# Decayed causal attention and a GELU MLP: one attention-times-values run per head pair, masks of batch 1 on GpSimd, and half a key block left out

## The chip, the cores and the metric

One core of a Trainium2 chip. The metric is the device time in microseconds (us) of one execution; "span" is the time from the first to the last instruction in a profile, 2 to 3 us less. Engines are TensorE (PE; its weight loads PEld), VectorE (DVE), ScalarE (ACT), GpSimd (POOL) and SyncE (SP), which issues transfers.

## The reference

```python
# q, k, v: (8 batches, 8 heads, 576, 64); f: (8, 8, 576)
scores = q @ k.T / sqrt(64)
cum = cumsum(log(clip(f, 1e-4, 1)))
scores = where(causal, -1e9, scores + cum[:, None] - cum[None, :])
attn = softmax(scores) @ v
x = attn.transpose(0, 2, 1, 3).reshape(8 * 576, 512)
out = gelu_exact(x @ w_in) @ w_out          # 512 -> 2048 -> 512
```

The decay is folded into v: each key's row of v is weighed by exp(-cum) and a 65th column carries the weights, so that softmax is a division by that column.

## The kernel before

Heads are worked on in pairs: a batch has pairs 0 to 3, each of two heads in the two halves of the partitions. A pair has four score tiles, scores(pair, 0..3), each followed by one exp on ScalarE and, from batch 2 on, by causal masks on GpSimd. "AV" is attention times values, 15 matmuls a head. A "bank" is a buffer in PSUM, the memory to which TensorE's results go; a matmul that needs a bank waits until the last user of it is done. Between these, TensorE takes single steps ("fill") of the second GEMM of the batch before.

```python
STILES = [
    [(0, 0, 256), (3, 384, 192)],          # (key block, first query, queries)
    [(0, 256, 320), (4, 448, 128)],
    [(1, 128, 448)],
    [(2, 256, 320)],
]
SDIAG = [[0, 256], [320], [0], [0]]        # columns of the diagonal blocks

s_psum = ctx.enter_context(tc.tile_pool(name="s_psum", bufs=2, space=PSUM))
o_psum = ctx.enter_context(tc.tile_pool(name="o_psum", bufs=2, space=PSUM))

    def scores(b, i, t):
        on_pe = b < 2                       # mask added by matmuls in batches 0 and 1
        st = s_psum.tile([P, 2, 512], FP32, tag="s", name=f"s{t}")
        # ... matmuls of 64 rows, both heads side by side ...
        et = e_pool.tile([P, 2, 512], BF16, tag=f"e{t}", name=f"e{t}")
        nc.scalar.activation(et[:, :, 0:c], st[:, :, 0:c], Act.Exp, scale=scale)
        for c0 in [] if on_pe else SDIAG[t]:
            nc.gpsimd.affine_select(out=et[:, :, c0 : c0 + P], ...)

    # second GEMM by token tile; "r": two 64-row matmuls side by side, "n": one of 128 rows
    PLAN = [
        (0, "o", 16 * "r"),
        (1, "m", 5 * "r" + 2 * "n" + 8 * "r" + "n"),
        (2, "m", 9 * "r" + 2 * "n" + 5 * "r"),
        (3, "s", 8 * "r" + 8 * "n"),
    ]
    FILL = [[6, 5, 4, 3], [0, 3, 3, 2], [0, 3, 3, 3], [0, 3, 3, 2], [8]]
    FILL_AV = [2, 1, 2, 2]

    def attention(b):                       # batches 2 to 7
        # ...
        counts = FILL_2 if b == 2 else FILL  # FILL_2: another list, not changed
        def av(i):
            for h in range(2):
                attend(b, i, h, (0, 1, 2, 3, 4))
                if h == 0 and (b > 2 or i == HP - 1):
                    take(fill, FILL_AV[i])
                normalize(b, i, h)
        for i in range(HP):
            for t in range(4):
                scores(b, i, t)
                take(fill, counts[i][t])
                if i and t == 1:
                    av(i - 1)
                # ...
                if t == 1 and i == 0:
                    load_v(b + 1)
        take(fill, counts[HP][0])
        if b == 2:
            to_xT(b, HP - 2, nc.vector.tensor_copy, o_psum, "o")
        av(HP - 1)
        take(fill, 5)
        to_xT(b, HP - 1, nc.vector.tensor_copy, o_psum, "o")
        # ...
    # main loop, first GEMM of batch b: v of batch b + 1 is weighed on GpSimd,
    # pair by pair, all four pairs ahead of the masks of batch b + 1
```

The softmax here doesn't subtract the row's maximum and nothing guards it: scores larger than these inputs give would overflow.

Of the kernel before, what the change touches and what calls it, by code (L numbers as in the profile page):

```python
# [9 lines left out]
BF16 = mybir.dt.bfloat16  # L10
Act = mybir.ActivationFunctionType
# [3 lines left out]
P = 128  # L15
S = 576
D = 64
H = 8
HP = 4
NBLK = 5  # L20
K0 = [0, 128, 256, 384, 448]
# [3 lines left out]
PT = 96  # L25


STILES = [
    [(0, 0, 256), (3, 384, 192)],
    [(0, 256, 320), (4, 448, 128)],  # L30
    [(1, 128, 448)],
    [(2, 256, 320)],
]

SDIAG = [[0, 256], [320], [0], [0]]


def where(n, m):

    q = K0[m]  # L40
    for t, parts in enumerate(STILES):
        c = 0
# [8 lines left out]
def kernel(  # L51
# [10 lines left out]
    nc = tc.nc  # L62
# [10 lines left out]
    scale = 1.0 / (D ** 0.5)  # L73
# [3 lines left out]
    consts = ctx.enter_context(tc.tile_pool(name="consts", bufs=1))  # L77
    qk_pool = ctx.enter_context(tc.tile_pool(name="qk", bufs=2))
    v_pool = ctx.enter_context(tc.tile_pool(name="v", bufs=1))
    e_pool = ctx.enter_context(tc.tile_pool(name="e", bufs=4))  # L80
# [50 lines left out]
    key_of = consts.tile([P, 2, P], BF16)  # L131
    after = consts.tile([P, 2, P], BF16)
    for t, op, fill in (
# [4 lines left out]
            out=t[0:D],  # L138
            in_=t[0:D],
            compare_op=op,  # L140
            fill=fill,
            base=0,
            pattern=[[-D, 2], [1, P]],
# [5 lines left out]
    make_identity(nc, ident_fp)  # L149


    qT = [consts.tile([P, S], BF16, name=f"qT{i}") for i in range(HP)]
    kT = [consts.tile([P, S], BF16, name=f"kT{i}") for i in range(HP)]

# [106 lines left out]
    e_of = {}  # L261

    def scores(b, i, t):
        on_pe = b < 2
        st = s_psum.tile([P, 2, 512], FP32, tag="s", name=f"s{t}")
        c = 0
        for n, q0, w in STILES[t]:
            masked = on_pe and c in SDIAG[t]
            for half in range(-1, 2 if masked else 0):
                for h in range(2):  # L270
                    d = slice(h * D, (h + 1) * D)
                    if half < 0:
                        to = st[:, h, c : c + w]
                        ab = kT[i][d, K0[n] : K0[n] + P], qT[i][d, q0 : q0 + w]
                    else:
                        last = (half + 1) * D
                        to = st[:, h, c : c + last]
                        ab = key_of[d, half, :], after[d, half, 0:last]
                    nc.tensor.matmul(  # L279
                        to, *ab, start=half < 0, stop=half == 1 or not masked  # L280
                    )
            c += w
        et = e_pool.tile([P, 2, 512], BF16, tag=f"e{t}", name=f"e{t}")
        e_of[b, i, t] = et
        nc.scalar.activation(et[:, :, 0:c], st[:, :, 0:c], Act.Exp, scale=scale)  # L285
        for c0 in [] if on_pe else SDIAG[t]:
            nc.gpsimd.affine_select(  # L287
                out=et[:, :, c0 : c0 + P],
                in_=et[:, :, c0 : c0 + P],
                compare_op=Alu.is_ge,  # L290
                fill=0.0,
                base=0,
                pattern=[[0, 2], [1, P]],
                channel_multiplier=-1,
            )

# [44 lines left out]
    def x_dma(b, i):  # L341
        nc.sync.dma_start_transpose(
            xT(b)[:, i, :].rearrange("d (m p) -> d m p", p=P),
            x_of[b, i].rearrange("p m h d -> p (m h d)"),
        )
# [31 lines left out]
    def gemm2(c):  # L377
# [35 lines left out]

    PLAN = [
        (0, "o", 16 * "r"),
        (1, "m", 5 * "r" + 2 * "n" + 8 * "r" + "n"),
        (2, "m", 9 * "r" + 2 * "n" + 5 * "r"),
        (3, "s", 8 * "r" + 8 * "n"),
    ]

# [8 lines left out]
    def gemm2_rows(c, plan):  # L429




        for ts, held, steps in plan:
            if held == "s":
                both = s_psum.tile([P, 2, d_model], FP32, tag="s", name="ps2")
                banks = [both[:, 0], both[:, 1]]
            else:
                pool = {"o": o_psum, "m": m_psum}[held]
                banks = [  # L440
                    pool.tile([P, d_model], FP32, tag=held, name="ps2")
                    for _ in range(2)
                ]
            ot = o_pool.tile([P, d_model], FP32, tag="ot", name="ot")
            for kt, step in enumerate(steps):
                last = kt == steps.rindex("r")
                for r in range(2 if step == "r" else 1):
                    rows = slice(r * D, (r + 1) * D) if step == "r" else slice(0, P)
                    nc.tensor.matmul(  # L449
                        banks[r],  # L450
                        g_of[c][kt][rows, ts * P : (ts + 1) * P],
                        w_out_sb[rows, kt, :],
                        start=(kt == 0),
                        stop=last if r else kt == n_ff - 1,
                    )
                if kt == n_ff - 1 if held == "s" else last:
                    nc.vector.tensor_copy(ot, banks[1])  # L457
                if kt == n_ff - 1:
                    nc.vector.tensor_tensor(ot, ot, banks[0], Alu.add)  # L459
                    store(c, ts, ot)  # L460
                yield
# [37 lines left out]
    def gemm2_third():  # L499
        yield from gemm2_half(0, 1)  # L500
        yield from gemm2_rows(0, PLAN_0)
        yield from gemm2_rows(1, PLAN_1)

    def take(gen, n):
        for _ in range(n):
            if next(gen, "end") == "end":
                return
# [89 lines left out]



    FILL = [[6, 5, 4, 3], [0, 3, 3, 2], [0, 3, 3, 3], [0, 3, 3, 2], [8]]  # L600
    FILL_AV = [2, 1, 2, 2]
    FILL_2 = [[8, 8, 8, 8], [8, 8, 4, 4], [4, 4, 4, 4], [4, 4, 4, 4], [8]]
    FILL_1 = [[0, 0, 0, 0], [0, 0, 0, 0], [0, 0, 2, 2], [2, 2, 0, 0], [4]]

    def attention(b):


        fill = gemm2_third() if b == 2 else gemm2_rows(b - 1, PLAN)
        counts = FILL_2 if b == 2 else FILL

        def av(i):
            for h in range(2):
                attend(b, i, h, (0, 1, 2, 3, 4))
                if h == 0 and (b > 2 or i == HP - 1):
                    take(fill, FILL_AV[i])
                normalize(b, i, h)

        for i in range(HP):
# [5 lines that stand above are left out]
                    if i < HP - 1 or b > 2:  # L624
                        x_dma(b, i - 1)
                if t == 1 and i == 0:
                    load_v(b + 1)
                if b > 2 and t == 0 and i < 2:
                    transpose_dma(b + 1, 4 * i, 4 * i + 4)
                if b == 2 and t == 1 and i == 1:  # L630
                    transpose_dma(3, 0, 4)
                    transpose_dma(3, 4, 8)
        take(fill, counts[HP][0])
        if b == 2:
            to_xT(b, HP - 2, nc.vector.tensor_copy, o_psum, "o")
        av(HP - 1)
        take(fill, 5)
        to_xT(b, HP - 1, nc.vector.tensor_copy, o_psum, "o")
        x_tail(b)
        take(fill, 999)  # L640

    def second_attention():


        b, fill = 1, gemm2_half(0, 0)

        def av(i, h):
            attend(b, i, h, (0, 1, 2, 3, 4))
            normalize(b, i, h)

        def transposes(i, pool, tag):
            for which in range(2):
                transposes_first(b, i, which, pool, tag)


        nc.scalar.activation(warm[0:1, 0:1], warm[0:1, 0:1], Act.Exp)
        weigh_v(1, 2)
        weigh_v(1, 3)
# [3 lines that stand above are left out]
                if i == 0 and t < 3:  # L662
                    transposes(t + 1, *((m_psum, "m") if t == 1 else (o_psum, "o")))
                take(fill, FILL_1[i][t])
                if i and t in (1, 2):
                    av(i - 1, t - 1)
                if i > 1 and t == 0:
                    to_xT(b, i - 2, nc.vector.tensor_copy, o_psum, "o")
                if (i, t) == (3, 0):
                    transpose_dma(2, 0, 4)  # L670
                    transpose_dma(2, 4, 8)
        to_xT(b, HP - 2, nc.vector.tensor_copy, o_psum, "o")
        av(HP - 1, 0)
        take(fill, FILL_1[HP][0])
        av(HP - 1, 1)
        both = s_psum.tile([P, 2, 1024], BF16, tag="s", name="ps_x2")
        take(fill, 99)
        gemm1_begin(1, both)
        x_tail(1)
        load_v(2)  # L680
# [69 lines left out]
```

## Time and profile before

| | before |
|---|---|
| time, median of 3 (low to high) | 353.64 us (353.11 to 353.71) |
| span of the profiled run, granted clock | 350.1 us, 0.998 |
| TensorE, ScalarE, VectorE, GpSimd busy | 96%, 62%, 54%, 35% of the span |
| start of scores(0, 0) in batches 1, 2, 3 | 39.97, 74.01, 121.30 us |
| period of batches 3 to 7 | 36.627 us |

The period is the mean of four distances between the first score matmuls of batches 3 to 7.

### The profile page before, as it was taken

To read this page: it belongs to the slowest core of one execution; us is meant where nothing else is said; L and a number is where in the kernel's file an instruction comes from. 1 tells how busy PE (TensorE), PEld (TensorE's weight loads), DVE (VectorE), ACT (ScalarE), POOL (GpSimd) and SP (SyncE) were. 2 spreads that over 40 slices of the span, in tenths; PEclk is the share of its full clock that TensorE was granted. 3 is DMA by queue.
4 is the path that set the end of the run, shared out by engine and by line. 5 is a ranking of instruction groups with operands and counts; after the bars stand their busy time and mean duration, and the time that the engine had idled before them with its cause. 6 is when DMAs were issued, how large, how long until landed. Compare 5 with 4: busy or idle time off the path is not lost.

```text
span 350.1 us, 8011 instructions
## 1 busy us (share of the span) xinstructions
PE 335.7 (96%) x3250; PEld 179.0 (51%) x3292; DVE 188.7 (54%) x424; ACT 215.6 (62%) x296; POOL 122.8 (35%) x237
## 2 busy tenths in 40 slices
PE   7799998999999999999999999999999999999995
PEld 3674565445554455545554455445544554444443
DVE  5670455943367935796469646975498452011011
ACT  5976785673734787468746874687567774603600
POOL 8390740209318044443436242714270530000000
PEclk9999999999999999999999999999999999999999
DMA  8999999993970989278944896299700150011013
GB/s 115 174 171 194 209 186 176 205 190 89 217 187 31 138 184 188 77 100 163 191 122 73 151 222 122 55 160 213 159 30 0 51 98 33 0 60 62 0 32 89
DMA packets 99924, 43.03 MB, mean 123 GB/s; under 512 B 78704, under 2 KB 95344, under 8 KB 99888
## 3 DMA queue, kind: packets, MB, share of 16 engines
q1 hardware_dynamic: 82592, 28.37, 40.4%
q0 software_dynamic: 16896, 13.63, 26.2%
q8 instruction: 25, 0.41, 0.5%
q10 hardware_dynamic: 400, 0.52, 0.4%
q14 instruction: 11, 0.09, 0.1%
HBM read 36.85 MB, written 9.44 MB: 132 GB/s over the span
## 4 chain that ended last, share of the span: by engine, by line
PE 83%; ACT 9%; issue 2%; POOL 2%; DMA 2%; DVE 1%; ACTq 0%; POOLq 0%; DVEq 0%
PE ps L358 35%; PE ps L449 20%; PE o L306 9%; PE ps L391 8%; PE s L279 7%; ACT e L285 5%; PE ps L484 2%; ACT L285 2%; DMA k<-in_k_dram 2%; ACT g L375 1%; PE ps_x L336 1%; POOL q L103 1%; DVE x L320 1%; POOL k L103 1%; PE ps_f L199 0%
## 5 line engine op out<-in xcount | busy, mean ns | idle before, releaser
L375 ACT ACTIVATE g<-ps 128x512 bf16<-128x512 f32 x144 | 85.3, 597 | 78.9 <-PE ps L358 78.9
L285 ACT ACTIVATE e<-s 128x896 bf16<-128x896 f32 (+1 forms) x128 | 104.4, 862 | 31.4 <-PE s L279 30.1
L358 PE MATMUL ps<-xT,w_in_sb 128*128 128x512 bf16 x503 | 111.9, 379 | 0.8 <-ACT ot L493 0.2
L449 PE MATMUL ps<-w_out_sb,g 64*128 64x512 bf16 (+1 forms) x726 | 103.3, 376 | 1.6 <-issue 0.8
L358 PEld LDWEIGHTS <-w_in_sb 128*128 128x128 bf16 x576 | 56.1, 98 | 67.5 <-issue 2.3
L287 POOL TENSOR_SCALAR_AFFINE_SELECT e<-e 128x256 bf16<-128x256 bf16 x120 | 47.6, 408 | 94.2 <-ACT e L285 93.4
L449 PEld LDWEIGHTS <-g 64*128 64x128 bf16 (+1 forms) x751 | 40.0, 94 | 30.8 <-issue 3.3
L279 PE MATMUL s<-qT,kT 64*128 64x320 bf16 (+4 forms) x384 | 47.0, 281 | 4.8 <-ACT e L285 3.4
L237 DVE COPY qT<-tq 64x288 bf16<-64x288 bf16 x96 | 48.5, 506 | 1.7 <-DMA tq<-q 0.3
L253 POOL TENSOR_TENSOR vw<-v_sb,wT 128x640 bf16<-128x640 f32 x31 | 39.7, 1279 | 22.2 <-DMA v_sb<-in_v_dram 22.1
L306 PEld LDWEIGHTS <-e 128*128 128x128 bf16 x960 | 35.7, 98 | 15.7 <-issue 9.1
L306 PE MATMUL o<-vw,e 128*128 128x65 bf16 x960 | 40.7, 194 | 0.7
L457 DVE COPY ot<-ps 128x512 f32<-128x512 f32 x26 | 17.9, 689 | 40.0 <-PE ps L449 40.0
L237 DVE COPY kT<-tk 64x288 bf16<-64x288 bf16 x96 | 33.1, 344 | 1.6
L279 PEld LDWEIGHTS <-kT 64*128 64x128 bf16 x384 | 20.4, 94 | 25.5 <-issue 12.6
L320 DVE TENSOR_TENSOR x<-o,r 128x320 bf16<-128x320 f32 x64 | 31.5, 491 | 2.4 <-DVE r L319 0.2
L400 DVE COPY ot<-ps 128x512 f32<-128x512 f32 (+2 forms) x9 | 5.7, 632 | 48.6 <-PE ps L391 45.8
L319 DVE RECIPROCAL r<-o 128x5 f32<-128x5 f32 x64 | 12.3, 192 | 29.3 <-PE o L306 29.1
L391 PE MATMUL ps<-w_out_sb,g 128*128 128x512 bf16 (+2 forms) x141 | 27.8, 355 | 0.2
L391 PEld LDWEIGHTS <-g 128*128 128x128 bf16 x144 | 13.5, 98 | 14.5
L459 DVE TENSOR_TENSOR ot<-ot,ps 128x512 f32<-128x512 f32 x26 | 17.9, 687 | 1.5
L348 POOL COPY tails<-xT 128x256 bf16<-128x256 bf16 x8 | 3.2, 398 | 41.8 <-DVE xT L339 41.8
(63 smaller groups left out, 164.3 us busy)
## 6 DMA issues: line engine op xcount, KB each, us to landing
out_dram<-ot SPq DMA_DIRECT2D x32, 256.0 KB, 2.2
v_sb<-in_v_dram SPq DMA_DIRECT2D x24, 256.0 KB, 4.8
q<-in_q_dram POOLq DMA_DIRECT2D x6, 576.0 KB, 6.0
k<-in_k_dram POOLq DMA_DIRECT2D x6, 576.0 KB, 8.6
v_sb<-in_v_dram SPq DMA_DIRECT2D x22, 128.0 KB, 5.2
w_in_sb<-in_moe_w_in_dram POOLq DMA_DIRECT2D x4, 512.0 KB, 7.2
w_out_sb<-in_moe_w_out_dram POOLq DMA_DIRECT2D x4, 512.0 KB, 12.0
q<-in_q_dram POOLq DMA_DIRECT2D x4, 144.0 KB, 4.3
```

What stands on the lines that cost most here:

```text
L237: nc.vector.tensor_copy(rows[:, odd], src[odd * D : (odd + 1) * D, 2 * i + h].rearrange("d j p -> d p j"),)
L253: eng.tensor_tensor(vw_of[b][:, hs, :, 0:D], v_sb[:, hs, :, :], w.unsqueeze(3).to_broadcast([P, 2, NBLK, D]), Alu.mult,)
L279: nc.tensor.matmul(to, *ab, start=half < 0, stop=half == 1 or not masked)
L285: nc.scalar.activation(et[:, :, 0:c], st[:, :, 0:c], Act.Exp, scale=scale)
L287: nc.gpsimd.affine_select(out=et[:, :, c0 : c0 + P], in_=et[:, :, c0 : c0 + P], compare_op=Alu.is_ge, fill=0.0, base=0, pattern=[[0, 2], [ ...
L306: nc.tensor.matmul(o[:, m, :], e_of[b, i, t][:, h, c : c + P], vw_of[b][:, 2 * i + h, n, :], start=(n == 0), stop=(n == m),)
L320: nc.vector.tensor_tensor(x_of[b, i][:, :, h, :], o[:, :, 0:D], r.unsqueeze(2).to_broadcast([P, NBLK, D]), Alu.mult,)
L358: nc.tensor.matmul(ps, w_in_sb[:, kt, ffb * P : (ffb + 1) * P], src[:, kt, 0:TC], start=(kt == 0), stop=(kt == n_dm - 1),)
L375: nc.scalar.activation(g_of[c][ffb], ps, Act.Gelu)
L391: nc.tensor.matmul(pss[ts][:, c0:c1], g_of[c][kt][:, ts * P : (ts + 1) * P], w_out_sb[:, kt, c0:c1], start=(kt == 0), stop=(kt == n_ff - 1),)
L449: nc.tensor.matmul(banks[r], g_of[c][kt][rows, ts * P : (ts + 1) * P], w_out_sb[rows, kt, :], start=(kt == 0), stop=last if r else kt == n ...
L457: nc.vector.tensor_copy(ot, banks[1])
```

## The change

Its intent: fewer interruptions of AV, less masking on TensorE, and no work on queries that the last key block never sees. The last block overlaps the one before it by 64 keys, so for its first 64 queries all that would be computed is masked or weighed with zero. Their part of the tile becomes constant zeros.

```diff
-    [(0, 256, 320), (4, 448, 128)],
+    [(4, 448, 128), (0, 256, 320)],
-SDIAG = [[0, 256], [320], [0], [0]]
+SDIAG = [[0, 256], [0], [0], [0]]
+    e4 = [consts.tile([P, 2, 448], BF16, name=f"e4{i}") for i in range(4)]
+    for t in e4:
+        nc.gpsimd.memset(t[:, :, 0:D], 0.0)
     def scores(b, i, t):
-        on_pe = b < 2
+        on_pe = b == 0 or (b == 1 and i == 0)
+            z = D if n == NBLK - 1 else 0
-                        to = st[:, h, c : c + w]
+                        to = st[:, h, c + z : c + w]
     # ... the operands and the masks by matmul likewise; et of t == 1 is one of e4 in turn ...
-        nc.scalar.activation(et[:, :, 0:c], st[:, :, 0:c], Act.Exp, scale=scale)
+        nc.scalar.activation(et[:, :, z:c], st[:, :, z:c], Act.Exp, scale=scale)
     # ... masks likewise from z on ...
-        (1, "m", 5 * "r" + 2 * "n" + 8 * "r" + "n"),
-        (2, "m", 9 * "r" + 2 * "n" + 5 * "r"),
+        (1, "m", 15 * "r" + "n"),
+        (2, "m", 16 * "r"),
-    FILL = [[6, 5, 4, 3], [0, 3, 3, 2], [0, 3, 3, 3], [0, 3, 3, 2], [8]]
-    FILL_AV = [2, 1, 2, 2]
+    FILL = [[6, 5, 4, 3], [0, 4, 3, 3], [0, 4, 3, 3], [0, 4, 3, 3], [8]]
-    FILL_1 = [[0, 0, 0, 0], [0, 0, 0, 0], [0, 0, 2, 2], [2, 2, 0, 0], [4]]
+    FILL_1 = [[0, 0, 0, 0], [0, 0, 0, 0], [2, 2, 2, 2], [2, 2, 2, 2]]
         def av(i):
-                if h == 0 and (b > 2 or i == HP - 1):
-                    take(fill, FILL_AV[i])
         av(HP - 1)
-        take(fill, 5)
+        take(fill, 6)
     # batch 1: no fill between and after the heads of the last pair
```

More of the change, by code (lines that the diff above doesn't have):

```diff
@@ L267, in scores @@
         for n, q0, w in STILES[t]:
+            z = D if n == NBLK - 1 else 0
             masked = on_pe and c in SDIAG[t]
             for half in range(-1, 2 if masked else 0):
+                if half == 0 and z:
+                    continue
                 for h in range(2):
@@ L272, in scores @@
                     if half < 0:
-                        to = st[:, h, c : c + w]
-                        ab = kT[i][d, K0[n] : K0[n] + P], qT[i][d, q0 : q0 + w]
+                        to = st[:, h, c + z : c + w]
+                        ab = kT[i][d, K0[n] : K0[n] + P], qT[i][d, q0 + z : q0 + w]
                     else:
                         last = (half + 1) * D
-                        to = st[:, h, c : c + last]
-                        ab = key_of[d, half, :], after[d, half, 0:last]
+                        to = st[:, h, c + z : c + last]
+                        ab = key_of[d, half, :], after[d, half, z:last]
                     nc.tensor.matmul(
@@ L282, in scores @@
             c += w
-        et = e_pool.tile([P, 2, 512], BF16, tag=f"e{t}", name=f"e{t}")
+        z = D if t == 1 else 0
+        if z:
+            et = e4[(b * HP + i) % len(e4)]
+        else:
+            et = e_pool.tile([P, 2, 512], BF16, tag=f"e{t}", name=f"e{t}")
         e_of[b, i, t] = et
-        nc.scalar.activation(et[:, :, 0:c], st[:, :, 0:c], Act.Exp, scale=scale)
+        nc.scalar.activation(et[:, :, z:c], st[:, :, z:c], Act.Exp, scale=scale)
         for c0 in [] if on_pe else SDIAG[t]:
             nc.gpsimd.affine_select(
-                out=et[:, :, c0 : c0 + P],
-                in_=et[:, :, c0 : c0 + P],
+                out=et[:, :, c0 + z : c0 + P],
+                in_=et[:, :, c0 + z : c0 + P],
                 compare_op=Alu.is_ge,
                 fill=0.0,
-                base=0,
-                pattern=[[0, 2], [1, P]],
+                base=z,
+                pattern=[[0, 2], [1, P - z]],
                 channel_multiplier=-1,
@@ L673, in second_attention @@
         av(HP - 1, 0)
-        take(fill, FILL_1[HP][0])
         av(HP - 1, 1)
         both = s_psum.tile([P, 2, 1024], BF16, tag="s", name="ps_x2")
-        take(fill, 99)
         gemm1_begin(1, both)
```

## The prediction

> **What bounds the kernel now.** I read the page's busy table first, then the 40 slices, then the chain that ended last in order of time, then timelines of TensorE, ScalarE, GpSimd and the transfer queue stage by stage.
>
> ```profile
> PE 335.7 (96%) x3250; PEld 179.0 (51%) x3292; DVE 188.7 (54%) x424; ACT 215.6 (62%) x296; POOL 122.8 (35%) x237
> ...
> DMA  8999999993970989278944896299700150011013
> ...
> L287 POOL TENSOR_SCALAR_AFFINE_SELECT e<-e 128x256 bf16<-128x256 bf16 x120 | 47.6, 408 | 94.2 <-ACT e L285 93.4
> L449 PEld LDWEIGHTS <-g 64*128 64x128 bf16 (+1 forms) x751 | 40.0, 94 | 30.8 <-issue 3.3
> L306 PE MATMUL o<-vw,e 128*128 128x65 bf16 x960 | 40.7, 194 | 0.7
> ```
>
> TensorE is the bound almost everywhere. Batches 3 to 7 repeat every 36.63 us (the last gelu starts at 158.03, 194.66, 231.28). The DMA row says something else about the start: the transfers are saturated (digits of 8 and 9) until about 79 us. Inside a steady batch, scores(pair 2, tile 1) waits for ScalarE:
>
> ```profile
> 203.17 0.59 PE L449 MATMUL ps<-w_out_sb,g 64*128 64x512 bf16 x4
> 203.62 0.37 PE L279 MATMUL s<-qT,kT 64*128 64x256 bf16 x4
> 204.22 0.37 PE L279 MATMUL s<-qT,kT 64*128 64x320 bf16 x4 [0.23 <-ACT e L285]
> ```
>
> The score tiles have two buffers, so this tile waits for the exp two tiles back. GpSimd in batch 2 is the other place to see:
>
> ```profile
> 61.62 0.40 POOL L348 COPY tails<-xT 128x256 bf16<-128x256 bf16 x1 [14.02 <-DVE xT L339]
> 64.55 0.84 POOL L103 DMA_DIRECT2D q<-in_q_dram  x1 [2.53 <-DMA tq<-q]
> 65.97 0.93 POOL L103 DMA_DIRECT2D k<-in_k_dram  x1 [0.59 <-issue]
> 78.55 1.28 POOL L253 TENSOR_TENSOR vw<-v_sb,wT 128x640 bf16<-128x640 f32 x1 [11.65 <-DMA v_sb<-in_v_dram]
> ...
> 83.91 0.23 POOL L259 CAST vw<-wT 128x10 bf16<-128x10 f32 x1
> 84.06 2.92 POOL L287 TENSOR_SCALAR_AFFINE_SELECT e<-e 128x256 bf16<-128x256 bf16 x8
> ```
>
> GpSimd waits 11.65 us for v of batch 2, weighs four pairs (4 x 1.38 us), and only at 84.06 starts the masks of pair 0. The first AV of batch 2 (attention times values) starts at 86.00 and needs the fifth mask, ending at 85.91, by its sixth matmul at 86.17. So there is 0.2 us of slack today, behind a transfer.
>
> **What the Trainium skill says.** "TensorE: Matmul & The Clock Gate", Back-to-back issue gap: N/2.4 + 2.5 ns when warm. The trace agrees: 512 columns start 215.5 ns apart. So 64 columns fewer save 27 ns; the two heads' 64-row matmuls run side by side and count once. "TensorEngine Tiling (Array Packing)", Key Properties: changing the tiling mode drains the array. The trace shows 93 ns: a 64-row second-GEMM step to the first 128-row AV matmul is 309 ns, 216 of them the step's own columns; AV to scores is 127 where AV to AV is 33. "ScalarE: Activation LUTs", What ACT_TABLE_LOAD costs: 0.833 ns an element, with overlap back to back. The trace has (915-704)/256 = 0.82, and a cadence of 814 for 896 elements; so 768 elements should take 810 ns, cadence 707. "GPSIMD Engine Reference", Performance versus the Vector engine: elementwise work there takes about twice as long. Here the same weighing takes 1279 against 828 ns, so 1.5 times, but that it is the slow place is right.
>
> **The change, part by part.**
>
> *Half of the last key block.* Removes 64 columns from one score tile per pair: 27 ns x 4 = 0.107 us of TensorE a batch; 107 ns of ScalarE a pair; a mask of 128x128 in place of 128x256 (290 for 408 ns, by the identity's select). The zeros are written once, early, while GpSimd waits 5.9 us for v: free.
>
> *One AV run per pair.* The order of instructions shows that in batches 3 to 7 the old fill between the two heads was already in 128-row mode (216 ns each, no drain). So no drain is saved; the steps move ahead of the AV run or to the end of the pair, and become two concurrent 64-row matmuls of the same 216 ns. What changes is where TensorE waits. From start times of batch 4:
> - up to scores(1,1): the wait there is for exp(0,3), which starts when its scores are done; 0.01 saved, the 27 ns vanish in the wait.
> - scores(1,1) to scores(1,2), 2.435: 4 fills + AV for 3 fills + 2 between heads: minus 0.216 - 0.027 = -0.242.
> - scores(1,2) to scores(2,1), 2.028: that is exp(1,2) starting 0.465 after, + 0.814 cadence + 0.755 to the release = 2.034, so ScalarE sets it. The extra fill goes into the wait (0.386 to about 0.17): 0.
> - scores(2,1) to (2,2): -0.027.
> - scores(2,2) to (3,1), 2.166: one row group lags 0.17 today because the add that frees its bank ends late; the add now starts earlier: -0.075.
> - scores(3,1) to (3,2): -0.242; from there to the end +0.216 - 0.018 (a small wait gone) = +0.197.
> Sum -0.40 a batch, five batches: -2.0 us.
>
> *Batch 2.* Its only fill between heads was two 64-row steps in the last pair, with two drains. But the second head's bank is freed by a VectorE copy:
>
> ```profile
> 102.66 0.48 DVE L339 COPY xT<-ps_x 128x640 bf16<-128x640 bf16 x1
> ```
> ```profile
> 101.87 0.64 PE L306 MATMUL o<-vw,e 128*128 128x65 bf16 x15
> 102.44 0.60 PE L449 MATMUL ps<-w_out_sb,g 64*128 64x512 bf16 x4
> 103.19 0.64 PE L306 MATMUL o<-vw,e 128*128 128x65 bf16 x15
> ```
>
> The second head starts 0.05 after that copy ends and cannot start sooner; taking the two steps away leaves TensorE idle for 0.8 us and the steps come later: +0.431. Score columns of pairs 2 and 3: -0.054.
>
> *Batches 0 and 1.* Batch 0: one shorter exp on the chain, 0.107, and 80 ns of columns and mask: -0.19. Batch 1: each diagonal mask on TensorE is 64 + 128 columns, 85 ns; five a pair, three pairs: 1.28 us of TensorE. Fifteen masks join GpSimd (about 0.34 each, 5 us in 10 us in which it is idle). The 16 fills move from the end (8 of them after the last scores) into the waits. I walked the stage by hand with the old durations: exp(1,2) from 46.79 to 46.57, scores(2,3) from 50.96 with 2 fills done to 51.20 with 6 done, the last transposes of x from 60.59 to about 59.2, after paying 0.5 for the last mask of pair 3. So batch 1 should give 1.4 us, and TensorE reaches the first AV of batch 2 1.6 us earlier, at about 84.4.
>
> There it meets GpSimd. The v transfer of batch 2 was issued at 63.43 behind transposing transfers that themselves wait for tokens landed at 51.82 and 54.47, in a saturated queue; nothing in that sequence waits for TensorE. So I leave the landing at 78.39 and the masks' start at 84.06. The shorter third mask ends the fifth at 85.79 instead of 85.91. AV waits, resumes its sixth matmul at 85.83, and scores(1,2) start at 86.74 instead of 87.04. Of the 1.6 us gained, 0.30 are left.
>
> Sum: -0.30 - 0.054 + 0.431 = +0.08 at the end of batch 2, then -2.0: -1.9. 353.64 - 1.9 = **351.7 us**.
>
> **The rivals.** First, the v transfer lands earlier, or the GpSimd queue is not what holds: then batches 0 and 1 keep 1.58 us, batch 2 costs 0.32, and the sum is -3.3: 350.4. For it: times of transfers in a saturated queue can shift when their neighbours do. Against it: its issue follows other transfers alone, and the mask's slack is 0.2 us. Second, joining the two heads starves VectorE: both heads are normalized back to back (2 x 0.72), and the last transposes come six steps after the AV run. I make x ready 2.08 after the start of the last run and TensorE there at 2.27, a margin of 0.19. If VectorE is later by 0.3, every batch loses 0.1 to 0.2: about 352.6. Third, TensorE's sum alone decides: then 0.107 x 8, 1.28 of masks, small change, 2.3 us in all: 351.3. It would be near in time, for a wrong reason. Fourth, the author's reading, that every head's interruption costs drains (2 x 0.093 x 4 pairs in six batches, 4.5 us more): 347 to 348. The instruction order speaks against it: 128-row fills stood between 128-row AV.
>
> **Range and chances.** The rivals span 350.4 to 352.6, apart from the fourth. Range 350.2 to 352.8. A gain of 2% needs 346.6 us; every mechanism I can name with its full size ends above that, so 0.03. Slower by 2% would need 7 us of new waits: 0.01. Same: 0.96.
>
> **What would show it.** In the profile after: the period of batches 3 to 7 near 36.2 us; the wait of scores(2,1) near 0.17; exp of 768 elements near 810 ns; the idle time of TensorE ahead of the first AV of batch 2 above 1 us, with v landing near 78.4; some 0.8 us between the two heads of the last pair of batch 2; batch 1's gemm starting near 59 us. I am wrong if the period stays at 36.6 (the fill did not go into the wait), if batch 2 starts its first AV without waiting, or if the steady batches lose drains that I say were not there.

## The result, and the profile after

| | before | after |
|---|---|---|
| time, median (low to high) | 353.44 us (353.11 to 353.71), 4 runs | 350.72 us (350.61 to 351.74), 4 runs |
| ratio, 95% interval | | 0.993 (0.9909 to 0.9951) |
| span of the profiled run | 350.1 us | 348.6 us |
| scores(0, 0) of batches 1, 2, 3 | 39.97, 74.01, 121.30 | 39.93, 72.53, 121.57 |
| period of batches 3 to 7 | 36.627 | 36.295 |

A ratio is the mean time of one kernel's fast runs over that of the other's of the same rounds, so not quite the ratio of the medians. By it the change is a gain of 0.7%: "within 2%".

The table already tells where the time went. Batch 2 began 1.47 us earlier, and batch 3 began 0.27 us later: between them 1.74 us were given back. After that each batch gained 0.332 us. The chain that ended last now runs through transfers and GpSimd, which before had 2% each (first line before, the others after):

```profile
PE 83%; ACT 9%; issue 2%; POOL 2%; DMA 2%; DVE 1%; ACTq 0%; POOLq 0%; DVEq 0%
PE 68%; DMA 10%; SPq 10%; ACT 4%; POOL 4%; issue 2%; DVE 0%; POOLq 0%; ACTq 0%; DVEq 0%
PE ps L370 28%; PE ps L461 20%; PE ps L403 8%; PE o L318 7%; SPq L117 7%; DMA v_sb<-in_v_dram 6%; PE s L287 5%; DMA k<-in_k_dram 3%; SPq L228 3%; POOL vw L258 2%; ACT e L297 2%; ACT L297 2%; ACT g L387 1%; PE ps_x L348 1%; POOL q L105 1%
```

Line 117 is the load of v and line 258 its weighing. TensorE's timeline at the first AV run of batch 2 shows the wait (columns: start, us from first start to last end, engine, line, instruction, count, and in brackets the idle time and its releaser):

```profile
84.72 0.23 PE L318 MATMUL o<-vw,e 128*128 128x65 bf16 x2
85.68 1.32 PE L318 MATMUL o<-vw,e 128*128 128x65 bf16 x28 [0.73 <-POOL e L299]
86.94 0.36 PE L287 MATMUL s<-qT,kT 64*128 64x448 bf16 x2
```

Two of the 30 matmuls run, then TensorE waits for a mask of GpSimd. The first two start 0.04 us apart, the third 0.92 after the second; start times within the group of 28 put another 0.28 us between the fifth and the sixth, where 0.03 is usual. So 0.89 and 0.25 us are waits. A third stands before the run and is not marked: the last fill step before it starts at 84.26 and is 0.216 us of columns, so TensorE was free at 84.47, and AV starts at 84.72, just after the first mask ends at 84.66: 0.24 us. (In the kernel before, the same step is followed by AV after 0.215 us.) GpSimd at that time, in its timeline:

```profile
60.15 0.40 POOL L360 COPY tails<-xT 128x256 bf16<-128x256 bf16 x1 [3.04 <-DVE xT L351]
...
78.75 1.28 POOL L258 TENSOR_TENSOR vw<-v_sb,wT 128x640 bf16<-128x640 f32 x1 [12.59 <-DMA v_sb<-in_v_dram]
...
84.11 0.22 POOL L264 CAST vw<-wT 128x10 bf16<-128x10 f32 x1
84.26 2.68 POOL L299 TENSOR_SCALAR_AFFINE_SELECT e<-e 128x256 bf16<-128x256 bf16 x8
```

It is done with batch 1's tail 1.5 us earlier than before (60.15 for 61.62) and starts on v 0.2 us later (78.75 for 78.55): the landing of the transfer did not move with TensorE, though its issue came 0.6 us earlier (62.84 for 63.43). At the end of batch 2, the second head of the last pair:

```profile
101.70 0.64 PE L318 MATMUL o<-vw,e 128*128 128x65 bf16 x15
103.03 0.64 PE L318 MATMUL o<-vw,e 128*128 128x65 bf16 x15 [0.69 <-DVE xT L351]
103.60 1.25 PE L461 MATMUL ps<-w_out_sb,g 64*128 64x512 bf16 x10
```

The second head starts 1.33 us after the first, where before it was 1.32 with two fill steps inside. The gap stayed and lost its contents. In a steady batch, the same place as in the prediction (batch 5):

```profile
202.53 0.81 PE L461 MATMUL ps<-w_out_sb,g 64*128 64x512 bf16 x6
203.18 0.74 PE L287 MATMUL s<-qT,kT 64*128 64x256 bf16 x8
203.74 0.83 PE L461 MATMUL ps<-w_out_sb,g 64*128 64x512 bf16 x6
204.72 1.11 PE L318 MATMUL o<-vw,e 128*128 128x65 bf16 x30 [0.16 <-issue]
```

Three fill steps (x6) stand before scores(2, 0) instead of two, and the idle time before scores(2, 1) is too short to be marked: the two groups of scores run together as x8. (Behind the "issue" before AV stands the one 128-row step of the plan, whose record is missing; its weight load is there. Some matmul records are missing in every trace, so this text uses start times and the program's counts.)

The new exp and mask, by shape (columns after the count: busy us, mean ns of one):

```profile
L297 ACT ACTIVATE e<-s 128x768 bf16<-128x768 f32 x32 | 25.8, 807 | 1.9 <-PE s L287 1.6
L299 POOL TENSOR_SCALAR_AFFINE_SELECT e<-e 128x128 bf16<-128x128 bf16 x27 | 7.9, 293 | 1.0 <-ACT e L297 0.7
```

### The profile page after: what moved, and what is told of

The parts are those of the page before. It is cut to its first block, busy times and chain, and to the rows that moved or that the text cites. A ratio compares the mean times of both kernels' runs of the same rounds, so it can differ in the third digit from the quotient of the medians.

```text
span 348.6 us, 7941 instructions
## 1 busy us (share of the span) xinstructions
PE 334.8 (96%) x3211; PEld 175.9 (50%) x3242; DVE 188.0 (54%) x424; ACT 212.8 (61%) x296; POOL 124.0 (36%) x256
## 4 chain that ended last, share of the span: by engine, by line
PE 68%; DMA 10%; SPq 10%; ACT 4%; POOL 4%; issue 2%; DVE 0%; POOLq 0%; ACTq 0%; DVEq 0%
PE ps L370 28%; PE ps L461 20%; PE ps L403 8%; PE o L318 7%; SPq L117 7%; DMA v_sb<-in_v_dram 6%; PE s L287 5%; DMA k<-in_k_dram 3%; SPq L228 3%; POOL vw L258 2%; ACT e L297 2%; ACT L297 2%; ACT g L387 1%; PE ps_x L348 1%; POOL q L105 1%
## 5 line engine op out<-in xcount | busy, mean ns | idle before, releaser
L297 ACT ACTIVATE e<-s 128x896 bf16<-128x896 f32 (+2 forms) x128 | 101.6, 837 | 32.6 <-PE s L287 30.9
L299 POOL TENSOR_SCALAR_AFFINE_SELECT e<-e 128x256 bf16<-128x256 bf16 (+1 forms) x135 | 49.2, 383 | 101.4 <-ACT e L297 101.1
L461 PEld LDWEIGHTS <-g 64*128 64x128 bf16 (+1 forms) x771 | 41.7, 94 | 36.2 <-issue 5.5
L287 PE MATMUL s<-qT,kT 64*128 64x320 bf16 (+4 forms) x384 | 46.0, 277 | 4.0 <-ACT e L297 2.6
L318 PE MATMUL o<-vw,e 128*128 128x65 bf16 x960 | 37.5, 194 | 2.7 <-issue 0.8
L318 PEld LDWEIGHTS <-e 128*128 128x128 bf16 x960 | 33.6, 98 | 12.1 <-issue 7.3
```

What stands on the lines that cost most here:

```text
L287: nc.tensor.matmul(to, *ab, start=half < 0, stop=half == 1 or not masked)
L297: nc.scalar.activation(et[:, :, z:c], st[:, :, z:c], Act.Exp, scale=scale)
L299: nc.gpsimd.affine_select(out=et[:, :, c0 + z : c0 + P], in_=et[:, :, c0 + z : c0 + P], compare_op=Alu.is_ge, fill=0.0, base=z, pattern=[[ ...
L318: nc.tensor.matmul(o[:, m, :], e_of[b, i, t][:, h, c : c + P], vw_of[b][:, 2 * i + h, n, :], start=(n == 0), stop=(n == m),)
L461: nc.tensor.matmul(banks[r], g_of[c][kt][rows, ts * P : (ts + 1) * P], w_out_sb[rows, kt, :], start=(kt == 0), stop=last if r else kt == n ...
```

## The experiments

The theory, from the prediction: (a) what batches 0 and 1 gain is lost at the first AV run of batch 2, because GpSimd weighs all four pairs of v after a transfer that does not depend on TensorE, ahead of the masks; (b) the last pair of batch 2 loses 0.43 us to a VectorE copy; (c) the steady batches gain because a fill step moves into a wait for ScalarE, not because AV is one run. Rivals: the transfer itself or something else holds batch 2; one AV run saves drains; the half block pays through its shorter exp.

The total times of this kernel scatter by up to 1% on the chips used here, most of it before batch 3, so every experiment is also read from its trace. Two rulers serve, shown together at the end of this section: the stretches of a steady batch, and the starts of batches 2 and 3.

### Again the changed kernel

> The changed kernel once more, as the base of the comparisons. Mine: 0.993 of the kernel before (some 2 to 2.7 us less), the period of batches 3 to 7 at 36.30 us, a wait of 0.9 us at the third and 0.25 us at the sixth matmul of the first AV run of batch 2. If the 0.7 us between the gain in the profiles' spans (1.5) and in the times (2.7) is scatter in when the v transfer of batch 2 lands, the profile of this run shows that wait longer or shorter with the landing.

Measured: 350.86 us (349.10 to 355.09, six runs, one of them slow), before 353.58 us (352.36 to 356.1, eleven runs); ratio 0.9912 (0.9871 to 0.9953). Period 36.297. The first AV run of batch 2 waited the same 0.89 and 0.25 us, and 0.55 instead of 0.24 before its first matmul, with v landed at 78.86 instead of 78.59 and all that follows 0.27 us later. So that run follows the landing one to one. The trace of the kernel before is one of its shortest (span 350.1; the eleven others 350.5 to 353.0, median 351.2, where the five fast runs of the changed kernel have 348.7), and it took 2.8 us beyond its span (352.91) where the changed kernel's took 2.0 (350.62). For both reasons the spans of the first two profiles differ by 1.5 us only.

### Weighing behind the first masks

```diff
-                if late == gap - 2:
+                if late == gap - 2 and (b > 1 or at == 0):
                     weigh_v(b + 1, at)
     # in attention(b), after scores(i, t) and its fill:
-                if t == 1 and i == 0:
+                if b == 2 and t == 3 and i == 0:
+                    for other in range(1, HP):
+                        weigh_v(2, other)
+                if t == (3 if b == 2 else 1) and i == 0:
                     load_v(b + 1)
```

> The changed kernel with the weighing of v for pairs 1 to 3 of batch 2 put behind the masks of its pair 0 on GpSimd, and the load of the next v behind that. If the GpSimd queue behind the v transfer holds the first AV run of batch 2 (mine): its waits of 0.89 and 0.25 us go, and the kernel is 1.1 us faster than the changed one (about 349.6 us), ratio 0.9967. If what batches 0 and 1 gained is lost to something else (the transfer itself, VectorE, the score tiles): 0.

Measured: 349.37 us (348.98 to 350.11), ratio to the kernel before 0.9879 (0.9849 to 0.991), against 0.9912 for the changed kernel beside it; the two intervals overlap, so it is the trace that decides. TensorE's timeline at the same place:

```profile
84.70 1.12 PE L318 MATMUL o<-vw,e 128*128 128x65 bf16 x30
85.75 0.36 PE L287 MATMUL s<-qT,kT 64*128 64x448 bf16 x2
```

All thirty matmuls in one piece, although v landed 1.5 us later in this run than in the changed kernel's (GpSimd's first weighing starts at 80.29). GpSimd's timeline shows why it no longer matters:

```profile
80.29 1.28 POOL L258 TENSOR_TENSOR vw<-v_sb,wT 128x640 bf16<-128x640 f32 x1 [13.02 <-DMA v_sb<-in_v_dram]
81.52 0.22 POOL L264 CAST vw<-wT 128x10 bf16<-128x10 f32 x1
81.67 1.72 POOL L299 TENSOR_SCALAR_AFFINE_SELECT e<-e 128x256 bf16<-128x256 bf16 x5
```

The five masks of pair 0 end 3.1 us after the first weighing starts (81.67 + 1.72 - 80.29), where in the changed kernel TensorE could resume its sixth matmul only 7.3 us after it (86.04 - 78.75). Batch 2 takes 47.62 us in place of 49.03 (120.38 - 72.76 against 121.57 - 72.53), so 1.41 us come back, of which 1.38 are the three waits (0.24, 0.89 and 0.25). The times also scatter less: 1.1 us from lowest to highest. Theory (a) holds, and the transfer itself does not hold the run.

### The same move in the kernel before

The same edit as above.

> The same move of the weighing in the kernel before. Mine: the first AV run of batch 2 there had 0.2 us of slack, so 0 (between -0.2 and +0.2 us). If the new order is worth something of its own: about -1 us here too.

Measured: 352.59 us (352.15 to 355.48), ratio 0.9993 (0.9952 to 1.0034). Batch 2 takes 47.30 us as before (47.29). The order of weighing is worth nothing until the change makes TensorE arrive earlier.

### Two steps back between the heads of batch 2's last pair

```diff
     # changed kernel, av(i)
                 attend(b, i, h, (0, 1, 2, 3, 4))
+                if b == 2 and i == HP - 1 and h == 0:
+                    take(fill, 2)
                 normalize(b, i, h)
-        take(fill, 6)
+        take(fill, 5 if b == 2 else 6)
```

> The changed kernel with two second-GEMM steps put back between the heads of the last pair of batch 2 alone. Mine: the second head starts at the same time, 0.05 us after the VectorE copy that frees its bank, the gap of 0.85 us there is filled, and the kernel is 0.43 us faster than the changed one. If one AV run saves two drains there (the rival): 0.2 us slower.

Measured: 350.89 us (349.28 to 353.13), ratio 0.9927 (0.9888 to 0.9967), not to be told from the changed kernel's 0.9912 in time. The trace tells it: from the first AV matmul of that pair to batch 3 it is 19.43 us, where the changed kernel has 19.87 and 19.86 in its two profiles. The heads start 1.32 us apart, as in all the others:

```profile
104.66 0.64 PE L318 MATMUL o<-vw,e 128*128 128x65 bf16 x15
105.22 0.60 PE L461 MATMUL ps<-w_out_sb,g 64*128 64x512 bf16 x4
105.98 0.64 PE L318 MATMUL o<-vw,e 128*128 128x65 bf16 x15 [0.15 <-DVE xT L351]
```

So (b) holds with its size, 0.43 us. What hid it in the time is a finding of its own. In this profile v landed at 79.92, 1.3 us later than in the changed kernel's first, and at the first AV run of batch 2 TensorE waited 0.98 us before the first matmul, then the usual 0.89 and 0.25 (by start times). Then the clock was halved (columns: stretch, length, busy us of PE, PEld, DVE, ACT, POOL, granted clock, DMA share, which sums over the packets and can pass 1, GB/s):

```profile
85.00:88.00 3.00, 1.37 (x26) 0.89 (x26) 1.22 (x3) 0.00 (x0) 3.00 (x10) 1.00 0.44 100
88.00:91.40 3.40, 3.40 (x27) 1.52 (x25) 1.18 (x4) 1.28 (x2) 0.68 (x3) 0.50 1.24 232
91.40:96.00 4.60, 4.44 (x65) 2.58 (x64) 2.06 (x5) 2.42 (x4) 1.46 (x4) 0.99 1.20 202
```

The half clock lasted from 88.03 to 91.45 by the trace's clock records; TensorE was busy throughout, and from the second head of that AV run to the next AV run it took 6.44 us, where the changed kernel has 4.82: 1.6 us lost. Two of this kernel's six runs have a mean clock of 0.995, and they are its two slowest (353.13 and 352.72). Runs of other kernels have such a clock too, the kernel before and its variant with the weighing moved among them, so the wait at AV is not the only way into it. A mean clock of 0.995 or less stands in 6 of the 24 runs of kernels with that wait, in 11 of the 47 listed runs of kernels with the old batch 1 and no such wait, and in none of the 11 of the two kernels with the changed batch 1 and no such wait. These counts do not show that the wait is the cause.

### One step moved, two AV runs kept

```diff
     # kernel before
-        (1, "m", 5 * "r" + 2 * "n" + 8 * "r" + "n"),
+        (1, "m", 5 * "r" + "n" + 9 * "r" + "n"),
-    FILL = [[6, 5, 4, 3], [0, 3, 3, 2], [0, 3, 3, 3], [0, 3, 3, 2], [8]]
+    FILL = [[6, 5, 4, 3], [0, 3, 3, 3], [0, 3, 3, 3], [0, 3, 3, 2], [8]]
-                    take(fill, FILL_AV[i])
+                    take(fill, 1 if i == 0 else FILL_AV[i])
```

> The kernel before with one edit: of the two second-GEMM steps between the heads of pair 0 one is moved to the end of pair 1's scores; two AV runs per pair stay. If what the steady batches gained is that step going into the wait of scores(2,1) for ScalarE (mine): the period of batches 3 to 7 falls from 36.627 by 0.216 to 36.41 us, the wait of scores(2,1) from 0.386 to 0.17, the kernel by 1.1 us. If it is the single AV run that pays (the rival): 36.63, no change.

Measured: period 36.406 us, 0.221 less, with two AV runs per pair. 351.77 us (351.54 to 352.42), ratio 0.9922 (0.9889 to 0.9955); the kernel before had 355.07 us in this call, with a mean clock of 0.995 or less in four of its seven runs, so ratios of this call flatter. The step moved into the wait is the gain, not the single run.

### The AV run and its plan alone

```diff
     # kernel before, batches 2 to 7: PLAN, FILL and av(i) as in the change,
     # FILL_AV gone, take(fill, 6) after the last AV; nothing else
```

> The kernel before with the single AV run per pair and its new fill plan alone (no half block, no masks moved). Mine: the period is that of the changed kernel less the three score tiles of 27 ns that count: 36.295 + 0.08 = 36.375 us; the end of batch 2 is 0.43 us later after its last AV run starts (19.87 for 19.43 us from the last pair's first AV to batch 3); together -0.8 us. If drains were saved: a period near 35.9 us.

Measured: period 36.380 us, and 19.86 us from the last pair's first AV to batch 3, both as expected. 352.16 us (351.07 to 352.56), ratio 0.9925 (0.9889 to 0.9961), flattering. It gains 0.247 us a batch, 0.221 of which the run before has shown to be the one moved step.

In this profile batch 2 began 1.4 us late, at 75.40, although batch 1 is untouched: within the first AV run of batch 1 TensorE stood for 1.2 us before the thirteenth matmul.

```profile
45.70 0.55 PE L306 MATMUL o<-vw,e 128*128 128x65 bf16 x12
47.43 0.27 PE L306 MATMUL o<-vw,e 128*128 128x65 bf16 x3 [1.18 <-issue]
```

The kernel before has 0.21 us there, at the same matmul, and two of its variants 0.38 and 0.41 (by start times, where this profile has 1.35); the variant with the half block alone has 0.96 within the second head. None of the seven profiles with batch 1's masks moved has it in that run. Without this wait batch 1 takes 33.82 to 33.83 us in four of the five profiles with the masks on TensorE, and 33.44 with the half block: it is the whole scatter of batch 1 there. "Issue" means that the profile shows nothing that TensorE waited for, and no run here settles what it is.

### Batch 1's masks and fill alone

```diff
     # kernel before
-        on_pe = b < 2
+        on_pe = b == 0 or (b == 1 and i == 0)
     # FILL_1 and the end of batch 1 as in the change
```

> The kernel before with batch 1's masks on GpSimd and its new fill alone. Mine: batch 2 begins 1.2 to 1.4 us earlier (74.0 to about 72.7), and the first AV run of batch 2 then waits for masks that end 7.5 us after v has landed, so that batch 3 begins within 0.3 us of before for the same landing; period unchanged at 36.63; time unchanged. If the masks moved are worth their TensorE time: -1.3 us.

Measured: batch 2 began at 72.80 instead of 74.01, and batch 3 at 121.58 instead of 121.30; v landed at 78.85 instead of 78.39. Period 36.623. 353.52 us (352.13 to 357.39), ratio 0.9986 (0.9917 to 1.0054). Its timeline at the first AV run of batch 2 has the wait of the changed kernel, with the old masks:

```profile
84.98 0.24 PE L306 MATMUL o<-vw,e 128*128 128x65 bf16 x2
86.06 1.33 PE L306 MATMUL o<-vw,e 128*128 128x65 bf16 x28 [0.84 <-POOL e L287]
```

So 1.2 us are gained on TensorE, and none of it reaches batch 3.

### The half block alone

```diff
     # kernel before: STILES, SDIAG, e4 and z in scores() as in the change; nothing else
```

> The kernel before with the half block alone. Mine: three score tiles a batch give 27 ns each, the fourth's vanish in a wait: period 36.627 - 0.08 = 36.55 us; about -0.5 us in all. If the shorter exp (107 ns a pair) were on the path of the steady batches: -0.4 us a batch.

Measured: period 36.546 us, 0.081 less: three tiles of 27 ns. The fourth and the shorter exp are worth nothing in a steady batch. 351.40 us (351.22 to 351.68), ratio 0.9909 (0.9871 to 0.9947), again against the slow-clocked runs of before; by the traces it is 0.5 us (349.6 for 350.1).

### The bank that is freed late

```diff
     # changed kernel
-        (1, "m", 15 * "r" + "n"),
+        (1, "m", 14 * "r" + 2 * "n"),
```

> The changed kernel with the plan of token tile 1 as fourteen 64-row steps and two 128-row ones (for fifteen and one), so that VectorE's copy of the second bank starts a step earlier. The term I mis-sized, scores(2,2) to scores(3,1), is 2.159 us after the change (2.034 if ScalarE alone set it) because one row group's bank is freed 0.168 us late. If that lag is what holds: 2.034, and the period 36.295 - 0.125 = 36.17 us. If the lag is not on the path: 2.159 and 36.295.

Measured: scores(2, 2) to scores(3, 1) is 2.028 us, and the period 36.167. 352.35 us (349.39 to 352.99), ratio 0.9935 (0.9889 to 0.998); two of the four runs have a clock of 0.995 and the time of its profile, without, is 349.39.

### All together, and the remaining waits filled

On the changed kernel: the weighing moved, the two steps put back, and

```diff
-        (1, "m", 15 * "r" + "n"),
+        (1, "m", 13 * "r" + 3 * "n"),
-    FILL = [[6, 5, 4, 3], [0, 4, 3, 3], [0, 4, 3, 3], [0, 4, 3, 3], [8]]
+    FILL = [[6, 6, 3, 4], [0, 3, 3, 4], [0, 3, 3, 4], [0, 3, 3, 3], [8]]
```

> All that the study points to on top of the change: weighing of batch 2 behind its first masks, two steps back between the heads of its last pair, token tile 1 as thirteen 64-row and three 128-row steps, and the fill of the steady batches moved to where TensorE waits for ScalarE (6, 6, 3, 4 in pair 0; 0, 3, 3, 4 in pairs 1 and 2; 0, 3, 3, 3 in pair 3). By the same hand working: per batch -0.095 to scores(1,1), three times -0.216, -0.125: period 36.295 - 0.87 = 35.43 us. With -1.1 and -0.43 for batch 2: 345 us. If ScalarE's chain cannot be hidden so: the waits stay and the period is above 36.0.

Measured: **344.71 us** (344.13 to 344.79, six runs), before 353.48 us; ratio **0.9731** (0.9701 to 0.976). Period 35.407. Its profile has nearly the same busy share of TensorE as the changed kernel, 96%, with less of it (330.3 us for 334.8):

```profile
PE 330.3 (96%) x3201; PEld 174.3 (51%) x3232; DVE 188.3 (55%) x424; ACT 211.6 (62%) x296; POOL 124.5 (36%) x256
```

All outputs were correct in every experiment.

### The two rulers

Stretches of batch 5, us, between the first matmuls of the score tiles named; "end" is the first of batch 6:

| | (0,0)-(1,1) | (1,1)-(1,2) | (1,2)-(2,1) | (2,1)-(2,2) | (2,2)-(3,1) | (3,1)-(3,2) | (3,2)-end |
|---|---|---|---|---|---|---|---|
| before | 5.198 | 2.435 | 2.028 | 2.218 | 2.166 | 2.435 | 20.144 |
| changed | 5.195 | 2.195 | 2.028 | 2.193 | 2.159 | 2.194 | 20.330 |
| before, one step moved | 5.197 | 2.220 | 2.029 | 2.215 | 2.168 | 2.435 | 20.143 |
| before, half block | 5.196 | 2.408 | 2.030 | 2.189 | 2.168 | 2.413 | 20.142 |
| changed, bank freed earlier | 5.197 | 2.195 | 2.028 | 2.193 | 2.028 | 2.196 | 20.330 |
| all together | 5.089 | 1.979 | 2.037 | 1.964 | 2.039 | 1.969 | 20.330 |

The third stretch never moves: ScalarE sets it. Whatever is taken out of the second and put in there is gained.

| | batch 2 begins | batch 3 begins | period | time (ratio) |
|---|---|---|---|---|
| before | 74.01 | 121.30 | 36.627 | |
| changed | 72.53 | 121.57 | 36.295 | 350.72 (0.993) |
| changed, again | 72.50 | 121.84 | 36.297 | 350.86 (0.9912) |
| changed, weighing moved | 72.76 | 120.38 | 36.299 | 349.37 (0.9879) |
| before, weighing moved | 74.64 | 121.94 | 36.625 | 352.59 (0.9993) |
| before, masks of batch 1 | 72.80 | 121.58 | 36.623 | 353.52 (0.9986) |
| all together | 72.86 | 120.05 | 35.407 | 344.71 (0.9731) |

## Why the prediction was right

The predicted 351.7 us against 350.72 and 350.86, in a range of 350.2 to 352.8; point by point:

- Batches 0 and 1: 1.58 us forecast, 1.47 measured at the start of batch 2. The sum fits partly by luck. Of batch 0's 0.19 us 0.04 are seen at the start of batch 1, which lies anywhere from 39.65 to 40.54 in the twelve profiles, so that term is not shown. Batch 1 gave 1.43 for the 1.4 forecast, but 0.21 of it is the unexplained wait within its first AV run, which I had not seen.
- The queue behind the v transfer: landing forecast at 78.39, measured 78.59; scores(1, 2) of batch 2 forecast at 86.74, measured at 86.94, later by just the landing's shift. TensorE was free for that run at 84.47, forecast about 84.4. The wait was shown to be GpSimd's order and not the transfer, and to be absent in the kernel before. The shortened masks took 293 ns on average (the third of this run 283) for the 290 I assumed.
- The copy that frees the bank: 0.43 us forecast and shown.
- The steady batches: 0.40 us forecast, 0.332 measured. Of the seven stretches six came within 0.015 us. The step that failed is "the add now starts earlier: -0.075"; it gave -0.007. The add does start earlier in the batch, but so does the step that needs its bank: the row group that needs it lags by 0.168 us where it had been 0.175. I had taken 0.726 us from the copy's start to the add's, which token tile 0 shows, where this tile has 0.80 in both kernels. Freeing the bank earlier gave 0.131 us a batch, so the lag was on the path as said, and its removal was the mis-sized term.
- "No drain is saved": right. The plan with one AV run gained 0.247 us a batch, of which 0.221 is one moved step with two AV runs.
- The first rival, that batches 0 and 1 keep their gain, would have been 350.4, nearer to the measured time than my sum. The runs reject its mechanism all the same. By the traces the change gains 1.5 us, less than my 1.9, and by the times 2.7. The measured difference is larger than the traces' for the two reasons given under "Again the changed kernel": the trace of the kernel before is a short one, and 0.8 us of the difference in time lies outside the spans. That the kernel before scatters upwards in its first 75 us is mostly the unexplained wait in batch 1 (batch 1 takes 34.04 to 35.17 us in the five profiles with all its masks on TensorE, 32.60 to 33.10 in the seven with them moved), and a late arrival costs the kernel before more: it has 0.2 us of slack at the AV run where the changed one waits for GpSimd in any case. That this is the whole of the remaining 1 us is argued, not shown.
- The second rival, VectorE starved by joined heads: the stretch from scores(3,2) to the next batch takes 20.330 us, where my sum says 20.341, so the late transposes lost nothing. The third, TensorE's sum alone, was at 351.3 also nearer in time than I was, by chance: with it batch 3 would have begun earlier, not 0.27 us later, and the period would have fallen by 0.107 us and not by 0.332.
- Two slips in the working change nothing: in the first rival batch 2 costs 0.377 us by the terms given (0.431 - 0.054), not 0.32, and the sixth matmul of the first AV run started at 86.16, not 86.17.

## What to carry to other kernels

Work taken off the bounding engine is worth what is left of it at the next thing that this engine waits for: before counting it, look for a transfer or a queue further on that does not move with it, and for the slack there. In an in-order queue, put only the work ahead of a first use that this use needs. Where two engines alternate, find the stretches that do not change length whatever is done, and move the bounding engine's free work into those; here that, and not fewer interruptions, took the steady period from 36.295 to 35.407 us, with 0.13 us of it from the bank that is freed earlier.

## What the Trainium skill lacked or had wrong

- "TensorEngine Tiling (Array Packing)", Key Properties, says that a change of tiling mode drains the array, without a size. Here it costs 92 to 96 ns each way between 64-row and 128-row matmuls.
- "TensorE: Matmul & The Clock Gate", Why this matters for your kernels, warns of idle gaps over about 3 us. Here waits of 0.98, 0.89 and 0.25 us within 2.3 us were followed, less than 1 us later, by half a clock for 3.41 us. Waits of 0.55, 0.89 and 0.25 us at the same place were not, in another profile. That the waits caused it is not shown: kernels without them had runs of low clock about as often.
- "ScalarE: Activation LUTs", What ACT_TABLE_LOAD costs, gives 186 + 0.833 ns an element. For 640, 768 and 896 elements that is 719, 826 and 932; measured 704, 807 and 918 in the changed kernel, about 2% less.
- "GPSIMD Engine Reference", Performance versus the Vector engine, says about twice VectorE's time for elementwise work. The weighing of v took 1279 ns against 828 (a single instruction on VectorE), a factor of 1.5.
- No page read has the cost of the causal mask on GpSimd: 405 ns for 128x256 and 293 ns for 128x128 bf16, and 0.36 us from one start to the next for the larger.
- A wait within the first AV runs of batch 1, at the thirteenth matmul or in the second head, of 0.21 to 1.35 us with no releaser in the profile: no page read and no run explains it.
